# Maxout from two weight differences: the first product goes to the output through w1 @ w_out, and the weights arrive as fp32

## The chip, the cores and the metric

The kernel runs on one core of one Trainium2 chip. The metric is the device time of one execution in microseconds (us). The engines are named as the profile names them: PE does the matrix multiplies (PEld is its weight load, which overlaps them), DVE is the vector engine, ACT the scalar engine, POOL the GpSimd, SP the engine that here only issues DMAs. Each engine works through its own queue in order, so an instruction that waits holds up all that is queued behind it on that engine.

## The reference

A gated linear attention with a recurrent state per head, then a feed-forward layer with three gates of which the largest is kept:

```
for t in range(768):                                   # 4 batches, 8 heads, head_dim 48
    state = alpha[t][:, None] * state + outer(k[t], v[t])
    y[t] = q[t] @ state
x = y as 3072 tokens x 384
h = max(max(x @ w1, x @ w2), x @ w3)                   # w1, w2, w3: 384 x 768
out = h @ w_out                                        # w_out: 768 x 384
```

All inputs and the output are fp32 in HBM.

## The kernel before

The work is cut into 12 steps (`NS`): three chunks of 256 tokens for each of four batches, step s being chunk s // 4 of batch s % 4. A step has two parts. The first is the recurrence in chunked form: load alpha, k, q and v of the step (384 KB each, into four rings of four buffers), logarithms and running sums of alpha, k and q scaled by the decays (`near_k`, `near_q`, `scaled`), transposes, scores, masked scores, the state update and the output y, kept in fp16 as `xT`. The second is the feed-forward part on `xT`: `gate` makes the products with w1, w2 and w3 for a group of 256 of the 768 columns (piece G with index 3 * group + g), `maxed` (piece h) folds them: g = 0 is a copy out of PSUM on ACT or DVE, g = 1 and g = 2 are each a maximum on DVE. `project` (O) multiplies by w_out and `store` (o) scales and sends out.

The order of all this is not found by a scheduler: `emit` runs through the string `ORDER`, one piece after the other, and every engine gets its instructions in that order. A piece is a letter, an index, possibly a letter for the engine (v DVE, p POOL, a ACT) and, behind the @, the step: `w0v@2` is `near_q` of step 2 on DVE. Loads (`l`) go out from SP's queue, or from ACT's with an a; stores and the DMA transposes (`D`) also from SP's. The weights come by piece K (`load_weight`, lines 102 to 109): nine loads of three 128 x 256 blocks of w1, w2, w3 and three of two 128 x 384 blocks of w_out, issued by POOL, which turn fp32 into fp16 on the way into `wcat` and `wo16`. H pieces are warm-up multiplies at the start. PSUM is eight banks, all of one tag.

Pieces that the prediction speaks of: K (`load_weight`), G (`gate`), h (`maxed`), O (`project`), w (`near_q`, `qa` in the profile), k and q (`scaled`, `qk`), S and s (state update `sps` and its sum `full`), z (`kept`), y (`st`), V (`vt`), Y (`attend`, `yps`), r (`inverse`, `ra`).

Of the kernel before, what the change touches and what calls it, by code (L numbers as in the profile page):

```python
# [23 lines left out]
def kernel(  # L24
# [29 lines left out]
    NQ = 4  # L54
    assert DM == H * D and NT == B * S and 2 * D == 3 * C and DM % P == 0
# [32 lines left out]
    wcat = cpool.tile([P, NF, 3, DF], FP16, name="wcat")  # L88
# [13 lines left out]
    def load_weight(_, i, *__):  # L102
        if i < 9:
            w = (moe_w1, moe_w2, moe_w3)[i % 3]
            src = w.rearrange("(f p) j -> p f j", p=P)[:, :, i // 3 * 2 * P:(i // 3 + 1) * 2 * P]
            nc.gpsimd.dma_start(wcat[:, :, i % 3, i // 3 * 2 * P:(i // 3 + 1) * 2 * P], src)
        else:
            src = moe_w_out.rearrange("(j p) m -> p j m", p=P)[:, 2 * (i - 9):2 * (i - 8)]
            nc.gpsimd.dma_start(wo16[:, 2 * (i - 9):2 * (i - 8)], src)
# [42 lines left out]
    def times(eng, dst, src, col):  # L152
# [6 lines left out]
     lps_of, dec_of, tps_of, aps_of, sps_of, gps_of, ops_of, full_of, kept_of) = ({} for _ in range(20))  # L159
# [211 lines left out]

    def gate(s, i, _):
        jg, g = i // 3, i % 3
        xT = xT_of[s]
        gps = bank([P, 2, U * P], f"gps{g}")
        for j in range(2):
            jj = 2 * jg + j
            for f in range(NF):
                nc.tensor.matmul(gps[:, j, :], wcat[:, f, g, jj * P:(jj + 1) * P],  # L379
                                 xT[:, f].rearrange("p u t -> p (u t)"),  # L380
                                 start=(f == 0), stop=(f == NF - 1))
        gps_of[s, i] = gps

    def maxed(s, i, eng):
        jg, g = i // 3, i % 3
        gps = gps_of.pop((s, i))
        if g < 2:
            h = work.tile([P, 2, U * P], FP16, name=f"h{g}", tag=f"h{g}")
# [10 lines left out]
    whole, left, right = slice(0, DM), slice(0, DM // 2), slice(DM // 2, DM)  # L399
    parts = {  # L400
        0: (0, range(NJ), {0: whole}), 1: (1, range(NJ), {1: whole}),
        2: (0, range(4), {0: whole}), 3: (0, range(4, NJ), {0: whole}),
        4: (1, range(4), {1: left, 2: right}), 5: (1, range(4, NJ), {1: left}), 6: (1, range(4, NJ), {2: right}),
    }

    def project(s, x, tag):
        u, jjs, outs = parts[x]
        for o, cols in outs.items():
            if jjs[0] == 0:
                ops_of[s, o] = bank([P, cols.stop - cols.start], "ops")  # L410
            for jj in jjs:
                nc.tensor.matmul(ops_of[s, o], hT_of[s][:, jj, u * P:(u + 1) * P], wo16[:, jj, cols],  # L412
                                 start=(jj == 0), stop=(jj == NJ - 1))

    def store(s, x, eng):
        c, b = divmod(s, B)
        u, cols = (1, (left, right)[x - 1]) if s == NS - 1 and x > 0 else (x, whole)
        ob = work.tile([P, DM], FP32, name="ob", tag="ob", bufs=5)[:, :cols.stop - cols.start]
# [4 lines left out]
    def warm(_, n, *x):  # L423
# [11 lines left out]
        "G": gate, "h": maxed, "O": project, "o": store,  # L435
    }

    def emit(order):
# [6 lines left out]
        l0@0 r0@0 H12@0 H4@0 H1@0 m0p@0 N0@0 c0@0 r1@0 l0@1 m0v@1 l2@0 H1@0 r0@1 f0@0 g0@0 H4@0  # L445
        w0p@0 l1@0 u0v@0 q0v@0 N0@1 c0@1 e0@0 l3@0 V0a@0 r1@1 e0@1 f0@1 l0@2 k1v@0 q1v@0 K1p@0
        M0p@0 l2@1 k0p@0 l1@1 K2p@0 K0p@0 k1p@1 m0v@2 w0v@1 H10@0 g0@1 N0@2 S0@0 s0a@0 T1@0
        t1a@0 c0@2 q1v@1 T0@0 z0p@0 f0@2 e0@2 g0@2 q0v@1 H1@0 l3@1 V0a@1 t0v@0 A1@0 A0@0 T1@1
        H2@0 u0v@1 a2@0 k0p@1 S0@1 T0@1 v1a@0 v0p@0 a1@0 a3@0 a0@0 Y0@0 Y2@0 t1v@1 K5p@0 y0p@0
        s0a@1 M0p@1 z0p@1 Y3@0 l0@3 v1a@1 t0v@1 m0v@3 A1@1 A0@1 x0a@0 x1a@0 G1@0 G2@0 l1@2 a2@1  # L450
        v0a@1 K3p@0 y0p@1 Y3@1 K4p@0 k1p@2 u0p@2 a1@1 N0@3 c0@3 a3@1 a0@1 Y0@1 r0@2 r1@2 x0v@1
        Y2@1 x1a@1 l2@2 s1v@0 s1v@1 f0@3 k0p@2 w0v@2 G0@0 l3@2 M0p@2 G1@1 G0@1 G2@1 h0a@0 q1v@2
        T1@2 g0@3 e0@3 h1v@0 V0a@2 S0@2 s0a@2 h0v@1 q0p@2 h1v@1 T0@2 t0a@2 t1v@2 G5@1 G5@0 K6p@0
        z0p@2 y0a@2 s1v@2 l0@4 v1p@2 h2v@0 h2v@1 r0@4 A1@2 A0@2 a0@2 G3@1 h3a@1 Y3@2 m0p@4 l3a@3
        a3@2 G3@0 N0@4 a1@2 K7p@0 v0p@2 l1@3 r0@3 G4@1 c0@4 g0@4 a2@2 Y2@2 x1v@2 h3a@0 Y0@2
        x0a@2 u0p@3 h4v@1 l0@5 G4@0 h5v@1 M1p@0 z1p@0 y1a@0 G0@2 h0a@2 G5@2 r1@3 G1@2 G3@2 h4v@0
        h5v@0 h1v@2 G2@2 l2@3 K8p@0 k0p@3 w0v@3 q0v@3 G6@2 V0a@3 h3a@2 l2@4 l1@4 r1@4 m0p@5
        M0p@3 h2v@2 G4@2 h4v@2 k1p@3 S0@3 s0v@3 N0@5 G6@1 h6a@2 h5v@2 r0@5 G7@2 h7v@2 T0@3 q1p@3
        T1@3 G7@1 K11p@0 z0p@3 e0@4 w0p@4 f0@4 l3@4 s1v@3 v0a@3 t1v@3 t0a@3 k1v@4 G6@0 h6a@1
        q1p@4 h7v@1 l2@6 u0p@4 c0@5 A0@3 a0@3 A1@3 T1@4 q0p@4 a2@3 G8@2 a3@3 h8v@2 G8@0 g0@5  # L460
        h6a@0 a1@3 f0@5 G8@1 K9p@0 k0p@4 T0@4 e0@5 h8v@1 G7@0 v1p@3 Y0@3 Y2@3 t1a@4 V0a@4 t0a@4
        h7v@0 K10p@0 y0p@3 Y3@3 x0a@3 x1a@3 l1@5 v1p@4 S0@4 A0@4 s0v@4 a1@4 A1@4 a3@4 M0p@4
        z0p@4 s1v@4 u0p@5 G0@3 l0@6 a0@4 G7@3 l1a@6 a2@4 v0v@4 y0a@4 m0p@6 r0@6 G3@3 h3a@3 G1@3
        G6@3 Y0@4 r1@5 l3a@5 h0v@3 Y3@4 h8v@0 Y2@4 x1v@4 N0@6 Y1@4 x0a@4 l2@5 G8@3 M1v@1 c0@6
        e0@6 f0@6 G0@4 h1v@3 k0v@5 q1v@5 G3@4 w0v@5 q0v@5 M0p@5 g0@6 u0v@6 r1@6 G1@4 l0@7 m0v@7
        G2@4 k1p@5 D1@5 h0a@4 z1p@1 k0p@6 O0@1 h1v@4 w0v@6 D0@5 q0p@6 D0@6 k1p@6 q1p@6 O1@1 N0@7
        l0@8 h6a@3 l3@6 h2v@4 l2@7 l1a@7 o1a@1 h7v@3 D1@6 h3v@4 o0a@1 V0a@5 O0@2 o0a@2 O1@2
        y1p@1 G7@4 h8v@3 S0@5 A0@5 s0v@5 o1a@2 a0@5 a1@5 A1@5 a3@5 a2@5 v1a@5 z0p@5 G4@4 v0p@5
# [6 lines left out]
        V0a@7 v1a@7 G0@6 h5v@5 M1v@4 z1p@4 G8@5 h2v@5 h3a@6 h7v@5 h4v@6 S0@7 h0a@6 v0p@7 l3@11
        o1a@0 h8v@5 y1a@4 A0@7 a1@7 s0v@7 u0p@8 A1@7 a2@7 m0p@9 a3@7 M0p@7 z0p@7 y0p@7 k0p@8
        Y1@7 a0@7 r0@9 l1a@9 G2@6 G1@6 h1v@6 q1p@8 G6@6 h6v@6 s1v@7 G5@6 Y0@7 Y2@7 N0@9 l2@9
        m0v@10 w0v@8 q0p@8 D0@8 Y3@7 k1v@8 D1@8 x0a@7 x1a@7 l3@9 G8@6 G7@6 r1@9 G6@7 h6a@7 G0@7
        V0v@8 c0@9 e0@9 O1@3 g0@9 M1p@5 u0v@9 k0v@9 O0@3 f0@9 w0p@9 G4@7 q1p@9 k1p@9 D1@9 q0p@9
        D0@9 o1a@3 o0a@3 V0a@11 h2v@6 h5v@6 h7v@6 h8v@6 G8@7 G7@7 h7v@7 h0a@7 S0@8 N0@10 s0v@8  # L480
# [6 lines left out]
        V0v@10 q0v@10 k0p@10 D0@10 O0@4 O1@4 g0@11 v0a@10 h7v@8 h2v@8 G4@9 h8v@8 G5@8 O1@7 r1@11
        v1p@10 S0@10 h3a@9 h4v@9 o0a@4 o1a@4 q1p@11 k1v@11 o1a@7 M1p@7 D1@11 s0v@10 A0@10 a0@10
        A1@10 a3@10 u0p@11 k0p@11 G7@9 z0p@10 y0a@10 y1p@6 G8@9 G3@8 h3a@8 O0@7 a1@10 w0v@11
        a2@10 h7v@9 h8v@9 Y3@10 Y1@10 Y0@10 Y2@10 G1@9 G0@9 x1v@10 x0a@10 G4@10 z1p@7 q0p@11  # L490
        D0@11 h4v@8 h0a@9 h5v@8 h1v@9 G2@9 G3@10 o0a@7 v1p@11 h2v@9 S0@11 s0v@11 A0@11 A1@11
# [43 lines left out]
```

## Time and profile before

| | us |
|---|---|
| median of 3 runs (152.74, 155.6, 153.05) | 153.05 |
| span of the profiled execution, first to last instruction | 150.5 |
| PE busy in it | 138.6 (92%) |
| DVE busy | 122.2 (81%) |
| ACT busy | 95.4 (63%) |
| POOL busy | 95.0 (63%) |

The profile is of one execution. Its span is 2.55 us below the median of the runs; that part lies before the first and after the last instruction. DMA moved 30.08 MB in 73033 packets, 65456 of them under 512 B; HBM reads are 23.69 MB. The 16 DMA engines are at 90% or more in most slices up to 47 us and again, less evenly, from 60 to 115 us. Names of tiles stand for what is computed: `gps<-xT,wcat` is a gate's product, `h` and `hT` are the folded gates, `ops<-wo,hT` the projection, `rq<-in_q_dram` a load of q.

### The profile page before, as it was taken

To read this page: it belongs to the slowest core of one execution; us is meant where nothing else is said; L and a number is where in the kernel's file an instruction comes from. 1 tells how busy PE (TensorE), PEld (TensorE's weight loads), DVE (VectorE), ACT (ScalarE), POOL (GpSimd) and SP (SyncE) were. 2 spreads that over 40 slices of the span, in tenths; PEclk is the share of its full clock that TensorE was granted. 3 is DMA by queue.
4 is the path that set the end of the run, shared out by engine and by line. 5 is a ranking of instruction groups with operands and counts; after the bars stand their busy time and mean duration, and the time that the engine had idled before them with its cause. 6 is when DMAs were issued, how large, how long until landed. Compare 5 with 4: busy or idle time off the path is not lost.

```text
span 150.5 us, 5517 instructions
## 1 busy us (share of the span) xinstructions
PE 138.6 (92%) x2301; PEld 105.9 (70%) x2301; DVE 122.2 (81%) x224; ACT 95.4 (63%) x199; POOL 95.0 (63%) x155
## 2 busy tenths in 40 slices
PE   6997589999798799999999999999899999999990
PEld 2445368778586588688886887678677788878660
DVE  5279788989999499999996999999699999566620
ACT  3588599575797576785969936788637344313071
POOL 8593999999779891799570976946589921000000
PEclk9999999999999999999999999999999999999998
DMA  5999999999996752999997996999996970011163
GB/s 127 319 317 278 263 239 278 250 271 271 283 248 155 103 135 80 193 227 284 214 245 182 332 331 163 201 178 339 281 246 158 146 95 31 4 52 57 52 235 131
DMA packets 73033, 30.08 MB, mean 200 GB/s; under 512 B 65456, under 2 KB 73008, under 8 KB 73008
## 3 DMA queue, kind: packets, MB, share of 16 engines
q1 hardware_dynamic: 59984, 24.12, 66.2%
q0 software_dynamic: 4416, 2.36, 11.9%
q10 hardware_dynamic: 8608, 3.25, 8.7%
q8 instruction: 18, 0.29, 0.8%
q14 instruction: 7, 0.06, 0.1%
HBM read 23.69 MB, written 4.72 MB: 189 GB/s over the span
## 4 chain that ended last, share of the span: by engine, by line
PE 49%; POOL 16%; DVE 9%; DMA 8%; issue 6%; SPq 5%; ACT 4%; POOLq 0%; DVEq 0%; ACTq 0%
PE gps L379 28%; PE ops L412 13%; POOL qk L222 5%; SPq L95 5%; DMA ra<-in_alpha_dram 4%; DMA rk<-in_k_dram 4%; PE yps L297 4%; DVE qa L193 3%; POOL st L150 2%; DVE h L396 2%; POOL kept L363 2%; PE aps L277 2%; POOL vu L150 2%; DVE hT L396 2%; POOL ka L189 2%
## 5 line engine op out<-in xcount | busy, mean ns | idle before, releaser
L379 PE MATMUL gps<-xT,wcat 128*128 128x256 f16 x648 | 76.5, 273 | 1.5 <-DVE hT L396 0.9
L379 PEld LDWEIGHTS <-wcat 128*128 128x128 f16 x648 | 61.5, 98 | 11.2 <-issue 1.9
L284 DVE TENSOR_TENSOR lat<-aps,cp 128x512 f16<-128x512 f32 x48 | 30.3, 681 | 0.7 <-PE aps L277 0.6
L396 DVE TENSOR_TENSOR h<-gps,h 128x512 f16<-128x512 f32 x36 | 24.6, 684 | 2.7 <-PE gps L379 1.2
L396 DVE TENSOR_TENSOR hT<-gps,h 128x512 f16<-128x512 f32 x36 | 24.1, 684 | 2.0 <-PE ops L412 1.3
L412 PE MATMUL ops<-wo,hT 128*128 128x384 f16 (+1 forms) x150 | 25.2, 320 | 0.0
L148 ACT CAST h<-gps 128x512 f16<-128x512 f32 x28 | 16.3, 584 | 9.1 <-PE gps L379 7.3
L412 PEld LDWEIGHTS <-hT 128*128 128x128 f16 x150 | 14.2, 98 | 7.8
L154 ACT ACTIVATE ob<-ops,c 128x384 f32<-128x384 f32 (+1 forms) x23 | 12.1, 567 | 11.5 <-PE ops L412 11.4
L363 POOL TENSOR_TENSOR kept<-full,gm 128x192 f32<-128x192 f32 x18 | 9.5, 532 | 11.1 <-DVE gm L335 5.0
L150 POOL COPY vu<-vt 64x384 f16<-64x384 f16 x24 | 12.2, 509 | 4.3 <-ACT vt L154 2.8
L148 ACT CAST xT<-yps 128x384 f16<-128x384 f32 x17 | 7.8, 480 | 8.4 <-PE yps L297 8.3
L154 ACT ACTIVATE vt<-rv,c 128x768 f16<-128x768 f32 x10 | 9.4, 940 | 4.9 <-DMA rv<-in_v_dram 4.9
L222 POOL TENSOR_TENSOR qk<-ka,ic 128x384 f16<-128x384 f32 x10 | 10.6, 1056 | 2.9 <-DVE ka L189 2.6
L426 PE MATMUL wps<-wo 128*128 128x512 f16 x35 | 10.6, 455 | 1.2 <-DVE wo L502 1.2
L148 ACT COPY vu<-vt 64x384 f16<-64x384 f16 x22 | 11.2, 509 | 0.3
L222 POOL TENSOR_TENSOR qk<-rq,ac 128x384 f16<-128x384 f32 x8 | 8.0, 998 | 1.5 <-DMA rq<-in_q_dram 1.4
L189 POOL TENSOR_TENSOR ka<-rk,ra 128x384 f32<-128x384 f32 x8 | 8.3, 1040 | 0.2
L277 PE MATMUL aps<-qkT 48*64 48x128 f16 x384 | 7.7, 219 | 0.8 <-DVE qkT L150 0.8
L148 ACT CAST st<-kept 64x192 f16<-64x192 f32 x18 | 6.3, 348 | 3.3 <-POOL kept L363 3.1
L297 PE MATMUL yps<-lat,vu 128*32 128x128 f16 x384 | 8.1, 220 | 0.1
L212 ACT ACTIVATE ac<-lps 128x384 f32<-128x384 f32 x12 | 6.0, 499 | 3.4 <-PE lps L200 3.4
(57 smaller groups left out, 194.6 us busy)
## 6 DMA issues: line engine op xcount, KB each, us to landing
ra<-in_alpha_dram SPq DMA_DIRECT2D x12, 384.0 KB, 5.5
out_dram<-ob SPq DMA_DIRECT2D x23, 192.0 KB, 2.1
rq<-in_q_dram SPq DMA_DIRECT2D x11, 384.0 KB, 6.2
rv<-in_v_dram SPq DMA_DIRECT2D x9, 384.0 KB, 6.6
rk<-in_k_dram SPq DMA_DIRECT2D x8, 384.0 KB, 7.0
wcat<-in_moe_w_dram POOLq DMA_DIRECT2D x9, 192.0 KB, 6.6
rk<-in_k_dram ACTq DMA_DIRECT2D x4, 384.0 KB, 4.4
rv<-in_v_dram ACTq DMA_DIRECT2D x3, 384.0 KB, 4.2
```

What stands on the lines that cost most here:

```text
L148: nc.scalar.copy(out=dst, in_=src)
L150: engines[eng].tensor_copy(out=dst, in_=src)
L154: nc.scalar.mul(dst, src, col)
L189: engines[eng or "p"].tensor_mul(near_of[s, "k"], raw("k", s, 0), raw("a", s, 1))
L222: engines[eng or "p"].tensor_mul(dst.rearrange("p a b c -> p (a b) c")[:, :, :D], near_of.pop((s, n)) if r == 0 else raw(n, s, r), dec_of[ ...
L277: nc.tensor.matmul(aps[i][r * J:(r + 1) * J, a * U + x, :], qkT[rows, r, 1, p, cols], qkT[rows, :, 0, p, cols], start=True, stop=True)
L284: nc.vector.tensor_mul(lat_of[s, u][:, i], aps_of[s, u][i], pmask.unsqueeze(1).broadcast_to([P, HP, P]))
L297: nc.tensor.matmul(y_of[s, x][C * m:C * (m + 1), f, :], lhs, rhs, start=(s, x, m) not in begun, stop=last[x] and n == len(todo) - 1)
L363: engines[eng or "p"].tensor_mul(kept, full_of.pop((s, x)), gm_of.pop((s, x)).unsqueeze(2).broadcast_to([P, HP, D]))
L379: nc.tensor.matmul(gps[:, j, :], wcat[:, f, g, jj * P:(jj + 1) * P], xT[:, f].rearrange("p u t -> p (u t)"), start=(f == 0), stop=(f == NF ...
L396: nc.vector.tensor_max(h, gps, h_of[s, i - 1])
L412: nc.tensor.matmul(ops_of[s, o], hT_of[s][:, jj, u * P:(u + 1) * P], wo16[:, jj, cols], start=(jj == 0), stop=(jj == NJ - 1))
```

## The change

Since max(a, b, c) = a + max(0, b - a, c - a), the output is x @ (w1 @ w_out) + max(0, x @ (w2 - w1), x @ (w3 - w1)) @ w_out. The change computes it so:

- `gate` has two products in place of three for each group of columns, with the differences in `wdif`; pieces G and h now have the index 2 * group + g.
- `maxed`: g = 0 is a positive part (Relu on ACT, maximum with 0 on DVE) instead of a copy, g = 1 one maximum on DVE; the third step is gone.
- `project` adds three products with `xT` and `w1o` ahead of the six with `hT` and `wo16`.
- `w1o` = w1 @ w_out is made on chip: 18 transposes of w1 (pieces B), three copies out of PSUM on DVE (n), 18 multiplies (P), three copies on ACT (p). They stand together just ahead of the first projection.
- the weights are loaded as fp32 from SP's queue into a pool `wst` of five buffers (`NW`), at the places in `ORDER` where POOL issued them before. The six differences are computed by DVE (three) and POOL (three), pieces d; ACT turns w1 and w_out into fp16 (b and C).
- buffers: `xT` 8 in place of 3, `h` 5 in place of two tags of 2, `ob` 4 in place of 5.

In `ORDER`, the pieces other than G, h and the new ones stand in the same sequence as before, on the same engines; of G and h those of the second gate (indices 1, 4, 7) are taken out and the others keep their sequence and engines. Pieces d stand just ahead of the first gate that needs them.

```diff
-    wcat = cpool.tile([P, NF, 3, DF], FP16, name="wcat")
+    wdif = cpool.tile([P, NF, 2, DF], FP16, name="wdif")
+    w1h = cpool.tile([P, NF, DF], FP16, name="w1h")
+    w1T = cpool.tile([P, NJ, DM], FP16, name="w1T")
+    w1o = cpool.tile([P, NF, DM], FP16, name="w1o")
...
-    def load_weight(_, i, *__):
+    def load_weight(_, i, eng):
+        staged = staged_of[i] = work.tile([P, 2 * NF * P], FP32, name="wst", tag="wst", bufs=NW)
         if i < 9:
             w = (moe_w1, moe_w2, moe_w3)[i % 3]
-            src = w.rearrange("(f p) j -> p f j", p=P)[:, :, i // 3 * 2 * P:(i // 3 + 1) * 2 * P]
-            nc.gpsimd.dma_start(wcat[:, :, i % 3, i // 3 * 2 * P:(i // 3 + 1) * 2 * P], src)
...
+            queues[eng].dma_start(staged.rearrange("p (f j) -> p f j", f=NF),
+                                  w.rearrange("(f p) j -> p f j", p=P)[:, :, i // 3 * 2 * P:(i // 3 + 1) * 2 * P])
...
+    def differ(_, i, eng):
+        jg, g = divmod(i, 2)
+        engines[eng or "p"].tensor_sub(
+            wdif[:, :, g, column_group(jg)], staged_of[3 * jg + 1 + g].rearrange("p (f j) -> p f j", f=NF),
+            staged_of[3 * jg].rearrange("p (f j) -> p f j", f=NF))
+
+    def halve(_, i, eng):
+        copy(eng or "a", w1h[:, :, column_group(i)], staged_of[3 * i].rearrange("p (f j) -> p f j", f=NF))
+
+    def turn_weight(_, i, tag):
+        wps_of[i] = bank([P, 2, NF, P], "tps", FP16)
+        for j in range(2):
+            for f in range(NF):
+                nc.tensor.transpose(wps_of[i][:, j, f], w1h[:, f, (2 * i + j) * P:(2 * i + j + 1) * P], ident)
+
+    def keep_weight(_, i, eng):
+        copy(eng or "v", w1T[:, 2 * i:2 * i + 2].rearrange("p j m -> p (j m)"),
+             wps_of.pop(i).rearrange("p j f m -> p (j f m)"))
+
+    def halve_out(_, i, eng):
+        copy(eng or "a", wo16[:, 2 * i:2 * i + 2].rearrange("p j m -> p (j m)"), staged_of[9 + i])
+
+    def multiply_weights(_, f, tag):
+        pps_of[f] = bank([P, DM], "pps")
+        for j in range(NJ):
+            nc.tensor.matmul(pps_of[f], w1T[:, j, f * P:(f + 1) * P], wo16[:, j], start=(j == 0), stop=(j == NJ - 1))
+
+    def keep_product(_, f, eng):
+        copy(eng or "a", w1o[:, f], pps_of.pop(f))
...
     def maxed(s, i, eng):
-        jg, g = i // 3, i % 3
+        jg, g = divmod(i, 2)
...
-        if g == 0:
-            copy(eng or "a", h, gps)
+        if g == 0 and eng == "v":
+            nc.vector.tensor_scalar_max(h, gps, 0.0)
+        elif g == 0:
+            nc.scalar.activation(out=h, in_=gps, func=AFT.Relu)
         else:
             nc.vector.tensor_max(h, gps, h_of[s, i - 1])
...
+    every = direct + through
...
-            for jj in jjs:
-                nc.tensor.matmul(ops_of[s, o], hT_of[s][:, jj, u * P:(u + 1) * P], wo16[:, jj, cols],
-                                 start=(jj == 0), stop=(jj == NJ - 1))
+            for what, j in terms:
+                lhs = xT_of[s][:, j, u] if what == "x" else hT_of[s][:, j, u * P:(u + 1) * P]
+                nc.tensor.matmul(ops_of[s, o], lhs, (w1o if what == "x" else wo16)[:, j, cols],
+                                 start=((what, j) == every[0]), stop=((what, j) == every[-1]))
```

The part of `ORDER` in which the new pieces first appear, before and after (`d`, `b` and the K without p are new; line breaks moved):

```
before: ... x0a@0 x1a@0 G1@0 G2@0 l1@2 a2@1 v0a@1 K3p@0 y0p@1 Y3@1 K4p@0 k1p@2 u0p@2 ... r0@2 r1@2 x0v@1 Y2@1 x1a@1 l2@2
        s1v@0 s1v@1 f0@3 k0p@2 w0v@2 G0@0 l3@2 M0p@2 G1@1 G0@1 G2@1 h0a@0 q1v@2 T1@2 ... G5@1 G5@0 K6p@0 ... l0@4 ...
after:  ... x0a@0 x1a@0 d1p@0 G1@0 l1@2 a2@1 v0a@1 K3@0 y0p@1 Y3@1 K4@0 k1p@2 u0p@2 ... r0@2 r1@2 x0v@1 Y2@1 x1a@1 l2@2
        s1v@0 s1v@1 f0@3 k0p@2 w0v@2 d0v@0 b0a@0 G0@0 l3@2 M0p@2 G0@1 G1@1 h0a@0 q1v@2 T1@2 ... d3p@0 G3@1 G3@0 K6@0 ... l0@4 ...
```

More of the change, by code (lines that the diff above doesn't have):

```diff
@@ L378, in gate @@
             for f in range(NF):
[L379 removed]
+                nc.tensor.matmul(gps[:, j, :], wdif[:, f, g, jj * P:(jj + 1) * P],
                                  xT[:, f].rearrange("p u t -> p (u t)"),
@@ L457 @@
[L457 to L468, printed above, removed]
@@ L475 @@
[L475 to L480, printed above, removed]
@@ L487 @@
[L487 to L491, printed above, removed]
-        a0@11 a3@11 h3a@10 G6@10 G0@10 M0p@11 z0p@11 G5@9 G1@10 y0v@11 a1@11 y1a@7 Y1@11 Y3@11
@@ new lines @@
+        h1v@5 h2a@6 S0@7 h0a@6 v0p@7 l3@11 o1a@0 h5v@5 y1a@4 A0@7 a1@7 s0v@7 u0p@8 A1@7 a2@7 m0p@9 a3@7
+        M0p@7 z0p@7 y0p@7 k0p@8 Y1@7 a0@7 r0@9 l1a@9 G1@6 q1p@8 G4@6 h4v@6 s1v@7 G3@6 Y0@7 Y2@7 N0@9 l2@9
+        m0v@10 w0v@8 q0p@8 D0@8 Y3@7 k1v@8 D1@8 x0a@7 x1a@7 l3@9 G5@6 r1@9 G4@7 h4a@7 G0@7 V0v@8 c0@9 e0@9
+        O1@3 g0@9 M1p@5 u0v@9 k0v@9 O0@3 f0@9 w0p@9 q1p@9 k1p@9 D1@9 q0p@9 D0@9 o1a@3 o0a@3 V0a@11 h1v@6
+        h3v@6 h5v@6 G5@7 h0a@7 S0@8 N0@10 s0v@8 O0@5 o0a@5 A0@8 a0@8 A1@8 a2@8 l0@11 Y1@8 G2@7 v1a@8 h2a@7
@@ new lines @@
+        O1@7 r1@11 v1p@10 S0@10 h2a@9 o0a@4 o1a@4 q1p@11 k1v@11 o1a@7 M1p@7 D1@11 s0v@10 A0@10 a0@10 A1@10
+        a3@10 u0p@11 k0p@11 z0p@10 y0a@10 y1p@6 G5@9 G2@8 h2a@8 O0@7 a1@10 w0v@11 a2@10 h5v@9 Y3@10 Y1@10
+        Y0@10 Y2@10 G0@9 x1v@10 x0a@10 z1p@7 q0p@11 D0@11 h0a@9 h3v@8 G1@9 G2@10 o0a@7 v1p@11 h1v@9 S0@11
+        s0v@11 A0@11 A1@11 a0@11 a3@11 h2a@10 G4@10 G0@10 M0p@11 z0p@11 G3@9 y0v@11 a1@11 y1a@7 Y1@11 Y3@11
+        v0a@11 a2@11 Y0@11 Y2@11 G1@10 x0a@11 G5@10 x1a@11 G5@11 G3@10 h3v@9 G3@11 h4a@10 h0v@10 G0@11
```

98 lines of the change are left out of this document (55 added, 43 removed).

## The prediction

> **What bounds the kernel now.** I read the page first, then the stretches of 5 us, then each queue in order of time. On the page PE leads, with the gates ahead of all else:
>
> ```profile
> PE 138.6 (92%) x2301; PEld 105.9 (70%) x2301; DVE 122.2 (81%) x224; ACT 95.4 (63%) x199; POOL 95.0 (63%) x155
> ```
>
> A mean over the span hides two regimes, which the stretches show (columns: PE, PEld, DVE, ACT, POOL, clock, DMA share, GB/s):
>
> ```profile
> 25.00:30.00 5.00, 4.73 (x106) 3.80 (x103) 4.97 (x9) 3.45 (x8) 4.86 (x7) 1.00 1.21 252
> 35.00:40.00 5.00, 4.41 (x69) 3.82 (x67) 4.96 (x5) 3.05 (x7) 4.98 (x7) 1.00 1.28 260
> ...
> 85.00:90.00 5.00, 5.00 (x93) 4.19 (x86) 5.00 (x10) 2.70 (x7) 4.30 (x8) 1.00 1.16 335
> 130.00:135.00 5.00, 5.00 (x43) 3.90 (x41) 2.19 (x4) 0.58 (x1) 0.00 (x0) 1.00 0.04 14
> ```
>
> Up to about 51 us (the front) DVE, POOL and the DMA engines are full and PE has gaps; from there PE has no gap in nearly every stretch, at a granted clock of 1.00. The chain of waits says where the front hands over (start, us, what), and gives the pace of PE:
>
> ```profile
> 50.86 0.35 POOL st L150
> 51.21 0.04 issue
> 51.26 0.35 PE yps L297 x11
> ...
> 91.64 1.97 PE ops L412 x12
> ...
> 134.25 4.58 PE gps L379 x42
> ```
>
> At 51.26 PE gets step 3's state from POOL. A gate multiply streams in 4.58/42 = 0.109 us, a projection multiply in 1.97/12 = 0.164.
>
> **PE's work.** 36 gate pieces of 6 multiplies go: 216 x 0.109 = 23.5 us. Added: three projection multiplies for each of 23 whole outputs and, for the halves, 6 half-wide ones (0.082): 69 x 0.164 + 0.5 = 11.8; 18 multiplies for w1 @ w_out, 3.0; 18 transposes at 0.46/8 = 0.058, 1.0. Over the whole kernel that is -7.7 us. But where it falls decides. Up to that point in `ORDER` the old program has 27 gate pieces and the new one 18, and none of the added work: 5.9 us leave the front, where PE already waits, so I count them at nothing. Behind it 27 pieces go, 17.7 us, and 15.8 come. The PE-bound part gains **1.9 us**, not 7.7. DVE loses 36 maxima of 0.684 (24.6 us); 27 of them lie where PE sets the time, so worth nothing.
>
> **The front.** Two things move here. DVE is relieved of 9 maxima (issued some 0.6 apart, 5.4 us) and gets three differences. POOL loses 12 DMA issues (7.3 + 2.3 = 9.6 us) and gets three differences of 768 columns, by its 384-column product (1.00) some 2.0 each. Alone that would make the front shorter. The other thing is SP. Its queue before (start, us until the issue was through):
>
> ```profile
> 14.21 4.02 SPq L95 DMA_DIRECT2D rq<-in_q_dram  x1
> 18.28 1.07 SPq L95 DMA_DIRECT2D rv<-in_v_dram  x1
> 19.53 1.00 SPq L95 DMA_DIRECT2D ra<-in_alpha_dram  x1
> ```
>
> The reader is to see that SP issues without a pause, held only by the DMA engines: a load takes about 1.2 us and all loads of the front are queued one behind the other until 44.8. Now weight loads stand in that queue and five staging buffers hold them. K1, K2, K0, K5, K3 take the five; K4 needs one back, and the first comes back when POOL has made d1. POOL makes d1 behind `kept` of step 1, at about 20.0 (that `kept` ran at 20.16 behind one weight issue more), until 22.0. So SP stands from 18.2 (16 issues at about 1.1) to 22.0, and behind K4 stand q and v of step 2, in the list above at 14.21 and 18.28. With the DMA engines run dry K4 lands at 24.9 (first load: issued 0.74, landed by 4.1 in the packet records) and q of step 2 one load later, 26.1; before it had landed by 21.5. DVE wanted it here:
>
> ```profile
> 24.54 0.82 DVE L193 TENSOR_TENSOR qa<-rq,ra 128x384 f32<-128x384 f32 x1
> 25.28 1.35 DVE L222 TENSOR_TENSOR qk<-rq,ac 128x384 f16<-128x384 f32 x1
> ...
> 37.16 2.83 DVE L193 TENSOR_TENSOR qa<-rq,ra 128x384 f32<-128x384 f32 x1
> ```
>
> So `w0v@2` goes to 26.4, +1.9. Right behind it is d0: its price is not in the trace; the nearest row is DVE's `qa` and `ka` of 384 fp32 columns, 0.55 alone, so 1.0 to 1.1 for 768, and 2.83 for 384 when POOL worked beside it. I take 1.0 here (POOL waits for that same `qa`), with 2.8 as the upper end. K6 waits for d0 (28.1), and behind K6 stand alpha of step 4, then K7, k of step 3, alpha of step 5, q of step 3: these land at about 32.2 to 36.7 instead of 27.6 to 32.7. G0 of steps 0 and 1 waits for d0 too, and with it `T1@2`, which stood at 26.69 and now comes near 30.2. Then d3 on POOL (28.2 to 30.2) holds G3, and d2 on DVE, behind the first masked scores of step 2 (about 35), holds G2. ACT has `h2a@1` behind G2, and behind that the load of v of step 3 (issued at 31.00 before, about 36.6 now) and `r1@3`, so `w0v@3` comes near 41 instead of 37.16 (it had waited for POOL until 40). By there DVE has been spared the maxima, which brings back most: `s0v@3` (41.71 before) comes near 43.8. The POOL chain from `z0p@3` (42.21) to `st` is 9.0 us; with d5 (+2.0) and without three issues of 0.76 (-2.3) and with one wait of DVE less sure it stays 9.0 to 9.4. The hand-over moves by 2.1 + 0.3 = **+2.4 us**. Ends: if the buffers come back in time, DVE's own balance, 5.4 - 3.0 = -2.4; with every difference of DVE at 2.8, +4.5. I take the chain above since each wait in it is written into the queues.
>
> In the page's rows a packet of 1 KB cast to 512 B on POOL's queue costs more than the plain one will (60 ns against 46, between 38 ns at 776 B and 65 at 1536 B in the packet records): 12 loads save some 3 us of DMA time, which the two dry spells of SP, about 2 us each, use up.
>
> [...]
>
> **Product and first projection.** B, n, P, p stand in one row on PE: P waits for DVE's copies (768 columns of fp16, between 0.55 and 0.68 by the rows of 384 and of 1024), and the last of the three comes 1.0 us after the last transpose; O0 waits for the last `p` (0.48 us by `xT`'s copy). With DVE in step that is 0.5 + 0.5 = 1.0 of gap, with DVE as far behind PE as at 60 us (its `ka`, `pa`, `h` run at 59.86 to 61.48, beside PE's projection at 60.19) 2.0 to 3.0. I take **+1.5**. The Relu costs what the copy did (0.584), the three fp16 conversions of ACT per kind (0.94 each by `vt`) lie in ACT's idle time; if ACT were late they would cost 0.9 apiece.
>
> Sum on the span: 150.5 + 2.4 - 1.9 + 1.5 = 152.5; with 2.55 outside the span **155.0 us**.
>
> **Rivals.**
> - *Forecast: the front gets later and eats the gain.* 155.0, own range 152.5 to 157.5. Chance 0.48.
> - *The staging buffers come back in time, or SP's stand stays hidden.* Front 0 to -2.4, product +1.0: 150.5 - 1.9 + 1.0 + 2.55 = 152.2 down to 149.8. For it: DVE is full in the front and loses work. Against: K4's wait on d1. 0.22. [...]
> - *PE sets the whole span.* All of -7.7 comes, product +1.0: 146.4. For it: 92% busy. Against: the gaps of the front. 0.08.
> - *The middle becomes bound by the recurrence, slower.* Counted piece by piece, PE's work between 51 us and the last output of step 11 (128 us) falls by 4.2 and rises by 2.3 behind it, where only PE works (POOL 0.00 at 130). If POOL's and SP's chain of step 5 to 11 paces the middle, the 4.2 turns into waiting and only the tail's +2.3 is left: 155.0 + 4.2 = 159.2. It makes the kernel slower by over 2% from 1.1 us of new gaps on. For it: SP waits 18.5 us for DVE ahead of its transposes; against: POOL is at 63% and DVE is relieved of 18 us there. 0.22.
>
> A measurement of this kernel can tell about 2% from no change, 149.99 to 156.11. Faster: all of the third, a tenth of the second and little else, 0.11. Slower: the fourth less a little, 0.20, and the upper part of the forecast, 0.14, makes 0.34. Same 0.55. The range for 8 in 10 leaves out the third case and the upper half of the fourth: 149.8 to 159.0.
>
> **What would show it.** Gate rows: 432 of about 273 ns; SP's queue with a stand of some 4 us ahead of the load of K4 that ends with POOL's first `wdif`, and one ahead of K6 that ends with DVE's; `rq` of step 2 as what DVE waits for near 26; PE's handover from POOL's `st` near 53.7; PE gaps of 1 to 2 us between the `w1T` copies and the first `ops`. Wrong it is if the chain has no SP or staging wait before 51 us, if DVE's `wdif` rows are far from 1.0, or if PE shows new gaps of over 2 us between 65 and 125 us.

## The result and the profile after

| | before | after |
|---|---|---|
| median of 4 runs, us | 153.15 (152.74 to 155.6) | 171.02 (170.5 to 171.18) |
| span of the profiled execution | 150.5 | 169.2 |
| mean granted clock of PE in it | 0.995 | 0.935 |

The ratio is 1.1182, with a 95% interval of 1.1149 to 1.1215: slower by 17.9 us. Some executions run some per cent longer than the others of their kernel, like the one of 155.6 here: the ratios and the medians of the experiments below leave them out, and a mark that is read from the profile of such an execution carries a ≤. PE does hardly more than before and all others but ACT do less, as the page of the profile shows (engine, busy us, share of the span, instructions), and the second line, the granted clock in 40 slices, has low stretches from 17 to 34 us and near 48 and 61:

```profile
PE 139.7 (83%) x2196; PEld 99.6 (59%) x2196; DVE 109.8 (65%) x194; ACT 100.9 (60%) x208; POOL 93.7 (55%) x146
...
PEclk9999567599978969999999999999999999999998
```

So the 18.7 us of the span are not added work: PE waits longer and, where its clock is low, takes longer for the same. To find where, I cut both spans at three marks that every version has: the end of the copy `xT` of step 3 (first half; the end of the front), that of step 5, and that of step 11. Before, then after (columns as in the stretches shown with the prediction):

```profile
0.00:50.60 50.60, 43.59 (x727) 31.20 (x727) 41.68 (x81) 36.48 (x74) 42.92 (x70) 1.00 1.10 249
50.60:69.50 18.90, 18.47 (x376) 14.74 (x377) 16.83 (x33) 12.53 (x28) 13.90 (x24) 1.00 0.77 166
69.50:128.60 59.10, 58.51 (x1061) 46.56 (x1059) 53.89 (x96) 39.99 (x87) 38.13 (x63) 1.00 0.95 209
128.60:150.50 21.90, 18.05 (x142) 13.44 (x140) 9.85 (x16) 6.36 (x13) 0.00 (x0) 0.97 0.25 91
```

```profile
0.00:62.60 62.60, 44.24 (x725) 30.54 (x729) 39.97 (x75) 40.04 (x80) 42.44 (x65) 0.84 0.85 242
62.60:86.70 24.10, 21.37 (x358) 15.04 (x347) 16.80 (x33) 14.45 (x33) 12.14 (x18) 1.00 0.73 185
86.70:145.00 58.30, 53.79 (x983) 39.82 (x981) 47.14 (x78) 39.89 (x87) 39.11 (x63) 1.00 0.79 186
145.00:169.20 24.20, 20.32 (x151) 14.23 (x149) 5.84 (x10) 6.56 (x13) 0.00 (x0) 0.97 0.23 82
```

The four stretches change by +12.0, +5.2, -0.8 and +2.3 us. The reader is to see two things. In the front PE's busy time is the same (43.6 and 44.2) and the length is not: it waits 18.4 us instead of 7.0. The busy time is the same although 54 gate multiplies fewer lie in it (108 instead of 162; at 0.109 they are 5.9 us), since the clock there is 0.84 instead of 1.00. In the third stretch, with the clock at 1.00 in both, PE's busy time falls by 4.7 us and the length by 0.8: PE had no gap there before, and lost work there bought almost nothing.

In the front the chain of waits shows the steps that the prediction spoke of, one after the other (start, us, what):

```profile
21.88 1.78 POOL wdif L384
...
23.67 0.37 SPq L112
...
24.08 4.15 DMA rq<-in_q_dram
...
28.33 0.06 DVE qa L200
...
28.80 0.96 DVE wdif L384
...
29.81 4.02 PE gps L419 x18
33.83 0.85 PE tps L263 x8
...
47.35 0.96 DVE wdif L384
...
48.35 1.46 PE gps L419 x6
49.82 0.61 PE sps L355 x18
...
55.52 1.81 POOL wdif L384
...
57.38 2.98 PE gps L419 x18
```

SP stands until POOL has made the first difference, and q of step 2 goes out only then. Three more differences, two of DVE and one of POOL, lie on the chain, each followed at once by a row of gates on PE, and the transposes (`tps`) and state products (`sps`) of the recurrence come behind those gates. The gates are slow, too: 18 multiplies in 4.02 us are 0.223 each, where the trace of before had 0.109, and PE's clock in stretches of 2.5 us says why:

```profile
17.50:20.00 2.50, 0.12 (x9) 0.12 (x12) 1.25 (x3) 1.08 (x2) 1.42 (x5) 0.51 1.11 307
20.00:22.50 2.50, 2.50 (x84) 2.25 (x83) 0.98 (x2) 2.43 (x6) 1.13 (x2) 0.50 0.72 207
22.50:25.00 2.50, 2.50 (x62) 1.68 (x52) 2.50 (x3) 2.26 (x6) 2.36 (x4) 0.62 0.11 20
```

The clock falls to a half at 17.55 us, in a stretch with 0.12 us of work, and stays there until 24.4 us (and again from 27.8 to 34.6, 48.3 to 51.7 and 58.5 to 61.9 us). The three rows of gates on the chain, 42 multiplies, take 4.02 + 1.46 + 2.98 = 8.46 us; at 0.109 each they would take 4.58, so 3.9 us of the chain are the low clock. The row at 22.50 also shows the DMA engines run dry (20 GB/s) while SP stands.

### The profile page after: what moved, and what is told of

Its sections match the earlier page's. It is cut to its first block, busy times and chain, and to the rows that moved or that the text cites. A ratio compares the mean times of both kernels' runs of the same rounds, so it can differ in the third digit from the quotient of the medians.

```text
span 169.2 us, 5268 instructions
## 1 busy us (share of the span) xinstructions
PE 139.7 (83%) x2196; PEld 99.6 (59%) x2196; DVE 109.8 (65%) x194; ACT 100.9 (60%) x208; POOL 93.7 (55%) x146
## 4 chain that ended last, share of the span: by engine, by line
PE 29%; DMA 19%; DVE 14%; ACT 12%; POOL 9%; issue 8%; SPq 7%; ACTq 0%; POOLq 0%; DVEq 0%
PE ops L458 13%; PE gps L419 10%; DMA rv<-in_v_dram 7%; DMA rq<-in_q_dram 6%; SPq L99 5%; DMA qkT<-qk 4%; DVE lat L291 3%; DMA ra<-in_alpha_dram 3%; POOL qk L229 3%; ACT vu L155 2%; SPq L112 2%; POOL wdif L384 2%; PE pps L407 2%; DVE qa L200 2%; ACT vt L161 2%
## 5 line engine op out<-in xcount | busy, mean ns | idle before, releaser
L419 PE MATMUL gps<-xT,wdif 128*128 128x256 f16 x432 | 56.9, 287 | 10.8 <-DVE wdif L384 7.2
L419 PEld LDWEIGHTS <-wdif 128*128 128x128 f16 x432 | 42.1, 102 | 20.2 <-DVE wdif L384 7.8
L458 PE MATMUL ops<-wo,hT 128*128 128x384 f16 (+1 forms) x150 | 27.5, 320 | 0.0
L436 ACT ACTIVATE h<-gps 128x512 f16<-128x512 f32 x28 | 16.4, 594 | 10.0 <-PE gps L419 8.9
L458 PE MATMUL ops<-w1o,xT 128*128 128x384 f16 (+1 forms) x75 | 16.0, 320 | 0.2 <-ACT w1o L155 0.2
L304 PE MATMUL yps<-lat,vu 128*32 128x128 f16 x384 | 9.2, 234 | 3.2 <-DVE vu L157 1.7
L284 PEld LDWEIGHTS <-qkT 48*64 48x64 f16 x384 | 6.4, 111 | 6.5 <-DVE qkT L157 2.3
L229 POOL TENSOR_TENSOR qk<-rq,ac 128x384 f16<-128x384 f32 x8 | 9.3, 1161 | 1.5 <-DMA rq<-in_q_dram 1.4
L304 PEld LDWEIGHTS <-vu 128*32 128x32 f16 x384 | 6.7, 104 | 4.7 <-DVE vu L157 1.9
L458 PEld LDWEIGHTS <-xT 128*128 128x128 f16 x75 | 6.9, 98 | 3.3
```

The source lines that it names most:

```text
L229: engines[eng or "p"].tensor_mul(dst.rearrange("p a b c -> p (a b) c")[:, :, :D], near_of.pop((s, n)) if r == 0 else raw(n, s, r), dec_of[ ...
L284: nc.tensor.matmul(aps[i][r * J:(r + 1) * J, a * U + x, :], qkT[rows, r, 1, p, cols], qkT[rows, :, 0, p, cols], start=True, stop=True)
L304: nc.tensor.matmul(y_of[s, x][C * m:C * (m + 1), f, :], lhs, rhs, start=(s, x, m) not in begun, stop=last[x] and n == len(todo) - 1)
L419: nc.tensor.matmul(gps[:, j, :], wdif[:, f, g, jj * P:(jj + 1) * P], xT[:, f].rearrange("p u t -> p (u t)"), start=(f == 0), stop=(f == NF ...
L436: nc.scalar.activation(out=h, in_=gps, func=AFT.Relu)
L458: nc.tensor.matmul(ops_of[s, o], lhs, (w1o if what == "x" else wo16)[:, j, cols], start=((what, j) == every[0]), stop=((what, j) == every[ ...
```

## The experiments

Five causes were to be told apart: the staging through SP; the gates that wait for a difference at the head of PE's queue (in some expectations theory D is its form in which the order alone decides); the half clock; the time of the differences themselves on POOL and DVE; and, behind the front, the product w1 @ w_out against a middle that PE does not pace. The marks of all kernels, in us of the span of the profiled execution; the last column is the median, the number of executions that it is taken from and, where there is one, the 95% interval of the ratio to before.

| | `xT` of step 3 | of 5 | of 11 | span | median (executions; ratio, 95%) |
|---|---|---|---|---|---|
| before | 50.6 | 69.5 | 128.6 | 150.5 | 153.05 (3) |
| after | 62.6 | 86.7 | 145.0 | 169.2 | 171.02 (4; 1.1149 to 1.1215) |
| e1_cast16 | 59.5 | 84.0 | 143.3 | 167.5 | 169.14 (2) |
| e2_warm | ≤62.8 | ≤86.8 | ≤144.1 | ≤168.3 | 167.48 (1) |
| e3_noprod | 62.0 | 80.6 | 140.8 | 165.2 | 166.93 (2; 1.0791 to 1.1033) |
| e4_beforeprod | 50.7 | 74.3 | 133.6 | 155.5 | 157.35 (2; 1.0172 to 1.04) |
| e5_front3 | 50.7 | 71.9 | 132.7 | 156.9 | 159.6 (4; 1.0399 to 1.051) |
| e6_late | 61.0 | 85.0 | 145.5 | 169.7 | 170.86 (2; 1.1096 to 1.1272) |
| e7_late16 | 63.8 | 88.1 | 149.7 | 174.0 | 174.76 (2; 1.1332 to 1.1546) |
| e8_twogates | 49.8 | 69.1 | 126.9 | 146.2 | 148.32 (4; 0.9654 to 0.9841) |
| e9_pack | ≤51.0 | ≤73.5 | ≤133.6 | ≤157.8 | 157.4 (3; 1.0238 to 1.0427) |
| e10_nowait | 56.1 | 82.2 | 142.7 | 167.0 | 168.71 (2; 1.0996 to 1.1128) |
| e11_latediff | 51.6 | 77.8 | 138.6 | 162.9 | 165.69 (2; 1.0726 to 1.095) |
| e12_beforediff | ≤56.1 | ≤77.3 | ≤137.1 | ≤159.0 | 158.14 (1) |

**The staging (e1_cast16).** The weights go back to POOL's queue and are turned into fp16 on the way, w1 into `w1h`, w2 and w3 into `wdif`, where the differences are made in place; the pieces b and C of ACT fall away.

```diff
-            queues[eng].dma_start(staged..., w...)
+            dst = w1h[...] if i % 3 == 0 else wdif[:, :, i % 3 - 1, column_group(i // 3)]
+            nc.gpsimd.dma_start(dst, w...)
...
-        tensor_sub(wdif[...], staged_of[3 * jg + 1 + g]..., staged_of[3 * jg]...)
+        tensor_sub(wdif[...], wdif[...], w1h[...])
```

> The weights arrive as before (POOL's queue, fp32 to fp16 on the way, no staging buffers); the two differences are taken in fp16, in place; ACT's conversions fall away; gates, product and projections are those of the changed kernel. Theory A (the front's 9 us come from fp32 weights in SP's queue behind five buffers, and what hangs on it): SP shows no stand before 45 us, the hand-over of step 3's state falls from 60.2 to 50 to 52 us, and the time to 157 to 162 us. Rival B (PE's clock, granted at about half in the front, would fall without the staging too): the clock rows stay at 0.5 to 0.8 between 20 and 35 us and the time stays above 165. Rival C (the product and the middle take most of the 18 us): the front is back but the time is 163 or more.

The front ends at 59.5 instead of 62.6: the staging, with all that goes with it, is worth 3.1 us, and 1.9 of the whole. The run does not single out SP's stand: the differences also get shorter in fp16 (DVE's 0.95 to 0.55, the first one 1.35; POOL's 1.81 to 1.63), ACT is spared its conversions, and POOL issues the loads again. It is the cause that the prediction had at its centre, and a quarter of the loss in the front. The clock fell without the staging too, to 0.67 from 20 to 25 us and 0.81 from 30 to 35 us, as rival B had it.

**The clock (e2_warm).** Warm-up multiplies are put ahead of the gates that wait, so that PE has something to do there.

```diff
-H2@0 ... G0@0 ... G2@1 ... G4@2 ... G4@1
+H14@0 ... H12@0 G0@0 ... H8@0 G2@1 ... H12@0 G4@2 ... H9@0 G4@1
```

> The changed kernel with warm-up multiplies put into the gaps that PE has ahead of S0 of step 1 and of the gates that wait for differences (12 more there, 12, 8, 12, 9; they add PE work and change no result). Rival B: the granted clock stays near 1.0 up to 65 us, 18 gate multiplies ahead of T1 of step 2 take 2.0 us instead of 4.0, and the time falls by 3 to 6 us, to 165 to 168. Theory A: the clock recovers but the waits on staged loads remain, so it falls by at most 3 us.

In the profiled execution (170.13 us) the mean clock rose from 0.935 to 0.970, though it was still 0.80 from 20 to 25 us and 0.78 from 30 to 35, and the front ended where it had, at 62.8. Between the copies of steps 1 and 3 it took 32.5 us instead of 35.1, but the added multiplies, which stand in PE's queue like all else, had cost the same ahead of that. The other execution, at a clock of 0.990, took 167.48, 3.5 us less than after; it has no profile. What the half clock costs thus stays open: 2.6 us in that part, 3.5 in the time, or the 3.9 by which it lengthens the gates on the chain. Where work fills the gaps, this run can't tell the clock from its cure.

**The product (e3_noprod, e4_beforeprod).** The first leaves the product out of after (first diff; pieces B, n, P, p; `w1o` is zero, so the output lacks the first product). The second adds it to before (second diff), its result unused.

```diff
-z1p@1 k0p@6 B0@0 B1@0 B2@0 n0v@0 n1v@0 n2v@0 P0@0 p0a@0 P1@0 p1a@0 P2@0 p2a@0 O0@1
+z1p@1 k0p@6 O0@1
```

```diff
-z1p@1 k0p@6 O0@1
+z1p@1 k0p@6 B0@0 B1@0 B2@0 n0v@0 n1v@0 n2v@0 P0@0 p0a@0 P1@0 p1a@0 P2@0 p2a@0 O0@1
```

> The changed kernel without w1 @ w_out: pieces B, n, P and p are left out and w1o is set to zero, so the first product's share of the output is left out. PE loses 18 transposes and 18 multiplies (3.9 us at full clock), DVE three copies, ACT three. If the product stands on the path with its waits, as forecast (3.9 + 1.5): 165 to 166 us. If the recurrence paces PE there anyway: 168 to 171.

> The kernel before with the product alone added at the same place (its result is not used): w1 from the fp16 weights, transposes, copies, multiplies. PE sets the time there, so at least its work of 3.9 us shows, and with the wait between B and P 4.5 to 6 us: 157.5 to 159. If DVE and ACT were the bound there: 154 to 156.

Without it the second stretch takes 18.6 us instead of 24.1, and the kernel 4.1 less; with it before takes 23.6 there instead of 18.9, and 157.35 against 152.53 in the same comparison, 4.8 more. The chain of after shows what it is made of: copies and multiplies that hand over to one another, the first output only behind them.

```profile
71.96 0.48 DVE w1T L157
...
72.49 3.39 PE pps L407 x18
...
75.90 0.49 ACT w1o L155
```

e3_noprod tells something else as well. From the end of the front to step 11 it has 140.8 - 62.0 = 78.8 us; before had 128.6 - 50.6 = 78.0. It has a third less of the gates, and three more products for each half of an output, and is not shorter.

**The order on PE (e6_late, e7_late16).** The recurrence's pieces are put ahead of the gates that wait for a difference, in after and in e1_cast16. The differences on DVE are moved back with their gates, and the load of v of step 3 goes out ahead of them.

```diff
-w0v@2 d0v@0 b0a@0 G0@0 l3@2 M0p@2 G0@1 G1@1 h0a@0 q1v@2 T1@2 ... T0@2
+w0v@2 b0a@0 l3@2 M0p@2 q1v@2 d0v@0 T1@2 ... T0@2 G0@0 G0@1 G1@1
...
-q0v@3 d4v@0 G4@2 V0a@3 ... S0@3 s0v@3 N0@5 G4@1 ... T0@3 q1p@3 T1@3
+q0v@3 V0a@3 ... S0@3 s0v@3 d4v@0 N0@5 ... T0@3 q1p@3 T1@3 G4@2 G4@1
```

> The changed kernel, staging and all, with the order alone altered in the front: gates of steps 0 to 2 that wait for a difference are put behind the recurrence pieces that stood behind them on PE (G1 of step 0 behind x of step 1; G0, G1 behind T0 of step 2; G3 behind A0 of step 2; G2 behind x of step 2; G4 behind T1 of step 3), the differences on DVE behind q, x and s in the same way, and the load of v of step 3 ahead of them. Theory D: the hand-over falls from 60.2 to 53 to 56 us (what the staging alone costs by the forecast is 2.4) and the time to 163 to 167. If the staged loads set the front: it stays above 58 and the time above 168.

> The same order as the last kernel with the weights by POOL's queue in fp16 and no staging, as in the first experiment. The difference to the last kernel is what SP's staged loads cost once the gates no longer hide it. Forecast's staging term: 2 to 3 us less than the last kernel, hand-over 51 to 53 us, time 161 to 165. If staging costs nothing at all: the same within 1 us.

This did not help: 61.0 and 63.8 at the end of the front, times of 170.86 and 174.76. By its own expectation e6_late would say that the staged loads set the front, but e7_late16, which has none, is 3.9 us slower still, which neither expectation had. The gates no longer stood ahead of the recurrence on PE, and the clock fell further, to 0.50 to 0.52 from 20 to 35 us in e6_late. In e7_late16 one difference met a run of POOL's instructions (DVE's queue, then the first and last of POOL's run: start, us, line, operation, tiles):

```profile
38.74 4.89 DVE L383 TENSOR_TENSOR wdif<-wdif,w1h 128x768 f16<-128x768 f16 x1
```

```profile
39.22 1.00 POOL L228 TENSOR_TENSOR qk<-ka,ic 128x384 f16<-128x384 f32 x1
...
42.23 0.98 POOL L228 TENSOR_TENSOR qk<-rq,ac 128x384 f16<-128x384 f32 x1
```

DVE's subtraction, 0.55 us at two of its three places in e1_cast16, lasts from 38.74 to 43.63, just past the end of POOL's run at 43.21. The order of PE alone was not the cause. Nor is what a wait at the head of PE's queue costs shown by these two runs, since the differences moved with the gates.

**The wait and the work of the differences (e10_nowait, e12_beforediff, e11_latediff).** e10_nowait is e1_cast16 with w2 and w3 in a tile of their own: the gates of steps 0 to 2 read them and wait for no difference, while the differences are still made at their places (for those steps the output has the raw gates). e12_beforediff is before with the six differences added at the same places, unused. e11_latediff is e10_nowait with all six on DVE: two of them early, in DVE's own gaps, the others later, at 43.4, 53.9, 57.1 and 59.2 us. The diffs stand in this order; of `ORDER` each shows a piece d with the piece beside it.

```diff
-                nc.tensor.matmul(gps[:, j, :], wdif[:, f, g, jj * P:(jj + 1) * P],
+                nc.tensor.matmul(gps[:, j, :], (w23 if s < 3 else wdif)[:, f, g, jj * P:(jj + 1) * P],
```

```diff
+        engines[eng or "p"].tensor_sub(wdif[:, :, g, cols], wcat[:, :, g + 1, cols], wcat[:, :, 0, cols])
...
+d1p@0 l1@2 ... d0v@0 l3@2 ... d3p@0 z0p@2 ... d2v@0 Y3@2 ... d4v@0 V0a@3 ... d5p@0 a3@3
```

```diff
-d1p@0 G1@0 ... d0v@0 G0@0 ... d3p@0 G3@1 ... d2v@0 G2@1 ... d4v@0 G4@2 ... d5p@0 G5@2
+d0v@0 t0v@1 ... d1v@0 x0v@1 ... d2v@0 k1v@4 ... s1v@4 d4v@0 ... v0v@4 d5v@0 ... x1v@4 d3v@0
```

> The first experiment's kernel (fp16 weights, no staging, two gates in every step) with one thing altered: the gates of steps 0 to 2 read the raw w2 and w3 instead of the differences (the subtraction is left out of these steps), so they need not wait for them; the differences are still made at the same places. Theory D1 (the waits on differences hold the recurrence): hand-over at 51 to 54 us and the time at 160 to 163 though PE has no more work in the front than in the changed kernel. Rival D2 (it is the missing work: PE idles without the third gate and its clock falls, whatever it waits for): the clock still falls to 0.5 to 0.8 and the hand-over stays above 57.

> The kernel before with the six differences alone added (fp16, from its fp16 weights, three on POOL, three on DVE, at the places in the order that they have in the changed kernel; the result is not used). All gates stay and none waits for a difference. If the differences' own time on POOL and DVE delays the recurrence of the front: x of step 3 at 53 to 56 us instead of 50.6 and 155 to 158. If DVE and POOL take them in their gaps: within 1 us of the kernel before.

> The last kernel but one of the same call's predecessor (gates of steps 0 to 2 read raw w2 and w3, so the subtraction is left out there; fp16 weights, two gates, no staging), with the six differences moved: all on DVE, two into gaps before 24 us, four behind 45 us, as in the fifth experiment. If the time that the differences take on DVE and POOL inside the front is what was left of the delay (x of step 3 at 56.1 there, 50.6 before): x of step 3 at 50 to 52.5 us and the time 3 to 6 us lower, 163 to 166. If it was the falling clock or the missing third gate: x of step 3 stays above 55 and the time above 167.

Taking the wait away brings the front from 59.5 to 56.1, 3.4 us, and the clock in the front from 0.86 to 0.94; the mark lies between what D1 and D2 expected. Of these 3.4 us only 0.4 remain in the time (168.71 against 169.14). The 5.5 us left over before are the differences' own: e12_beforediff, which has all three gates and nothing that waits for the differences, ends its front at 56.1 as well at most (its time is 5 us above before's), and e11_latediff, which differs from e10_nowait in nothing but who makes them and where, at 51.6; 3.0 of these 4.5 us remain in its time (165.69 against 168.71). So the front is not the whole loss: e11_latediff has it back but for 1.0 us and is still 8.4% slower than before. Its second stretch takes 26.2 us where before has 18.9, 5.5 of that by the product; the other 1.8 are not explained. The chain of e10_nowait shows how the differences get in although no gate waits for them:

```profile
44.00 0.55 DVE wdif L384
...
50.82 1.63 POOL wdif L384
...
53.18 1.00 POOL qk L229
```

The last one lies between two of POOL's instructions for the recurrence and moves the second by its whole length.

**The front given back (e5_front3, e9_pack).** e5_front3 keeps the algebra but lets steps 0 to 2 use three gates as before, in the order of before, with two of the differences in DVE's gaps, at 18.5 and 22.8 us, and four from 49.5 us on; the product is made ahead of the first output that needs it, its transposes before `O1@0`. The weights come as in e1_cast16. e9_pack has the product's pieces earlier and spread out between those of the recurrence of steps 4 and 5, and its first copies on ACT.

```diff
-        jg, g = divmod(i, 2)
+        jg, g = divmod(i, 3 if s < 3 else 2)
...
-                nc.tensor.matmul(gps[:, j, :], wdif[:, f, g, jj * P:(jj + 1) * P],
+                nc.tensor.matmul(gps[:, j, :], (w1h[:, f, jj * P:(jj + 1) * P] if s < 3 and g == 0 else
+                                                 w23[:, f, g - 1, jj * P:(jj + 1) * P] if s < 3 else
+                                                 wdif[:, f, g, jj * P:(jj + 1) * P]),
...
+        if s < 3:
+            terms = through
```

> Steps 0 to 2, whose gates fill PE in the front, take their three gates from w1, w2 and w3 as the kernel before (weights by POOL's queue as before, six-term projections for these steps); from step 3 on the differences are used, taken on DVE long before the first gate that needs them; the product stands later, its copies ahead of the sixth projection pair. Theory D (in PE's queue the recurrence of steps 2 and 3 stands behind gates that wait for differences, and PE idles and loses its clock there): the hand-over of step 3's state is back at 51 to 52 us, the clock at 1.0 throughout, and the time falls by 9 us and more, to 155 to 160. Rival B' (the half clock alone): the same time, but then the warm kernel should have gained most of it, which it did not. Rival E (the recurrence paces the middle: steps 5 to 11 take 59 us in every kernel so far): from the end of step 5's x to that of step 11's again 59 us, so that less PE work there brings nothing; if PE paced it, 54 to 56 us.

> The kernel with three gates in steps 0 to 2 (fifth experiment), with the product put into gaps that PE has there: transposes ahead of Y0 of step 4 (a gap of 1.5 us at 55.6), the copies on ACT instead of DVE, the multiplies ahead of S0 and A0 of step 5 (gaps of 0.6 and 1.4 us). If the product costs what does not fit into gaps: 2.5 to 3.5 us less than that kernel, 155 to 157. If the recurrence around it takes the time anyway: the same within 1 us. Either way above the kernel before.

The front of e5_front3 is before's, 50.7 us, and its mean clock there is 1.00. It takes 159.6 us all the same: what is left of the change behind the front costs 4.5%. e9_pack, at 157.4, is the fastest version of the algebra found here, 2.2 us below e5_front3 where 2.5 to 3.5 had been expected. No version that beats before was found, and this was no search.

**Who paces the middle (e8_twogates).** Before, with the products with w2 left out in all steps (pieces G and h 1, 4 and 7 are out of `ORDER`, the output is made from the larger of two, `h0` has 5 buffers); no work is added.

```diff
-            nc.vector.tensor_max(h, gps, h_of[s, i - 1])
+            nc.vector.tensor_max(h, gps, h_of[s, i - 2])
```

> The kernel before with the second gate left out (the products with w2 and their maxima, indices 1, 4 and 7 of each step; h0 gets five buffers so that they last to the third gate), nothing else: PE loses 23.5 us of work and DVE 24.6. If PE paced the kernel behind the hand-over, the 17.7 us behind it go: 135 to 138. Theory E (the recurrence paces the middle as closely as PE did): the front stays at 50.5 to 52, x of step 5 to x of step 11 stays at 57 to 59 us, only the gates behind the last output go (8.5 / 3 = 2.8 us) and a little before: 148 to 151.

216 multiplies (23.5 us of PE at before's pace) and 36 maxima (24.6 us of DVE) go, and the time falls from 152.34 in the same comparison to 148.32, by 4.0. Of the 4.3 us on the span 0.8 lie in the front, 1.3 in the third stretch, 2.6 behind step 11, where POOL is done (and 0.4 are lost in the second). In the third stretch PE now has 6.2 us of idle time where it had 0.6:

```profile
69.10:126.90 57.80, 51.57 (x953) 37.86 (x951) 45.21 (x78) 39.63 (x87) 38.77 (x61) 0.94 0.88 210
```

So in a middle in which PE was busy at 99% something else took nearly as long. The chain of before does not show it, since it runs along PE there (gates are 40% of it between 69 and 130 us). The low clock in this row, 0.94, is not what held the length: e5_front3 has 1.00 in its third stretch, PE idle for 4.6 us, and takes 60.8 us. The chain of after points to what it may be (start, us, what):

```profile
116.97 0.58 ACT ob L161
...
120.26 0.14 SPq L467
...
120.45 5.72 DMA rq<-in_q_dram
...
126.23 1.00 POOL qk L229
...
137.28 3.20 DMA qkT<-qk
...
140.52 0.44 PE aps L284 x15
```

SP sends out a scaled output, then the load of q queued behind that store; POOL scales, a DMA transposes, PE gets its scores. Between the first and the last of these lines, 24 us, the chain has no line of PE, so no gate. Whether loads ahead of the stores would shorten it was not tried.

## Why the prediction was wrong

It forecast 155.0 us with a range to 159.0, and the time was 171.02. On the span the miss is 16.7 us: 9.6 in the front (+12.0 for +2.4; the forecast counted to POOL's `st`, which came 6.5 late, and the mark, the copy of step 3, lies behind it) and 7.1 from there to step 11 (+4.4 for -2.7, which is the fall of 4.2 in PE's work and the +1.5 for the product). The tail, +2.3, came as counted.

**The front, its first steps: right in kind, short in size.** SP stood ahead of K4 until POOL's difference (forecast 22.0, measured 23.67) and ahead of K6 until DVE's; q of step 2 landed at 28.2 (26.1; in before at 21.8); d0 took 0.95 (1.0); `T1@2` came at 33.83 (30.2). These are late by 1.7 to 3.6 us. The first 1.7 come in part from v of step 1, which with three weight loads now ahead of it in SP's queue landed at 18.9 (before 16.8); 2.0 of the 3.6 are the gates ahead of `T1@2`, 18 in 4.02 us, which the forecast had put at the full clock. That "SP issues without a pause, held only by the DMA engines" is not what the profile of before says: it puts 13.8 us of SP's waits up to 48 us down to POOL, ACT and DVE. The step back to POOL's queue in e1_cast16, with all that it changes, gave 3.1 us; that this is near the forecast's +2.4 is chance, since that number was a sum of other terms.

**The front, the step that failed: "By there DVE has been spared the maxima, which brings back most".** This was the term that took the forecast from 41 us for `w0v@3` back to 43.8 for `s0v@3`, 2.1 us later than before; they came at 44.80 and 50.41, 7.6 and 8.7 later. So the 1.7 us that were to come back between the two did not, and 1.1 more were lost. The relief of DVE by 5.4 us was counted, but DVE's load was not what the chain ran through. Two prices were missing. A gate that waits for its difference holds the state products and transposes that stand behind it in PE's queue: 3.4 us (e1_cast16 against e10_nowait; the clock is in it, and the two runs with another order did not bring it back). The prediction named the waits of G0, G2 and G3, and `T1@2` behind the first, but not `S0@3` (the `sps` at 49.82 in the chain above), which stood behind G4, nor `T0@4` and `Y0@3`, which stood behind G5 until 60.36, so that the copy of step 3 comes 3 us later against the hand-over than before (PE's queue: start, us, what, and in brackets the idle time before it and what ended it):

```profile
48.35 1.46 PE L419 MATMUL gps<-xT,wdif 128*128 128x256 f16 x6 [2.80 <-DVE wdif L384]
```

And six differences were put between the recurrence's own instructions on POOL and DVE, at a moment when those engines pass work back and forth: 5.5 us (e10_nowait against before, net of what two gates instead of three save; with e11_latediff for the place). The forecast priced single ones rightly (1.8 to 2.1 on POOL for 2.0, 0.95 on DVE for 1.0) and took them as paid by the spared maxima and DMA issues. The three parts, 3.1, 3.4 and 5.5, are those of one order of undoing them; in another order they might divide otherwise. They are lengths of the front, not of the time: of the 11.0 us that e11_latediff has back there, 5.3 show in its time. The last stretch, from `z0p@3` to `st`, was right again: 9.3 us for 9.0 to 9.4. The end of the range for the front, +4.5, came from raising the durations of DVE's differences to 2.8, and those were not the trouble.

**The middle: rival 4 came true and more.** "From there PE has no gap" was read as "PE sets the time". Of the fall in PE's work up to step 11 nothing came (e3_noprod: 78.8 us for 78.0), as that rival had it with 4.2 us; the trace even held what spoke for it, and it was given 0.22. The test by removal (e8_twogates) makes it plain: 99% busy and 89% busy (51.57 of 57.80) took the same time within 1.3 us. Which chain it is that takes as long, the rival's of POOL and SP or another, was not tested by a run of its own.

**The product: right in its sum.** 4.0 us of work and 1.5 of gaps make 5.5, which were 5.5 in its stretch (e3_noprod; 4.6 of PE's busy time and 0.9 of gaps) and 4.1 to 4.8 in the whole time; e3_noprod loses part of its gain again in the third stretch, which takes 60.2 us instead of 58.3.

**What would show it.** Gate rows of 273 ns at the median, 432 of them: so it was. The hand-over from POOL's `st` stood at 60.2, not 53.7. Of the signs that would make it wrong, "new gaps of over 2 us between 65 and 125 us" was the right one to name; they came as many small ones, 4.5 us in the third stretch.

## What to carry to other kernels

An engine without gaps need not be what sets the time (PE was busy at 99% in the third stretch of before, which with a third of the gates gone got shorter by 1.3 us): take work away from it and look at the length of the stretch before counting a saving on it. New work in a front where engines pass a recurrence back and forth can cost most of its length at the place where it stands, however idle the mean (six differences of 7.4 us in all cost 5.5 in e10_nowait); put it where the trace of that engine has a gap, or behind the hand-over (e11_latediff has 4.5 of them back), and keep what waits for it off the head of a queue that the recurrence needs (3.4 us of the front, e1_cast16 against e10_nowait). Price a wait by everything queued behind it, on the issuing queue (q of step 2 behind SP's wait until 23.67) and on the consumer's (`S0@3` behind G4 until 49.82).

## What the hardware did that was not expected

Between 5 and 165 us PE's granted clock changed in after at 17.55, 24.38, 27.79, 34.62, 48.27, 51.68, 58.51 and 61.92 us, 3.41, 6.83 or 13.65 us apart, each a whole multiple of 3.41. Each fall to a half came behind a stretch of 3.41 us of that grid in which PE was busy for 1.62, 1.73, 0.69 and 1.19 us; stretches with 1.83 (from 65.34 us) and 1.97 (from 10.72) left it at 1.00, and before, on the grid of its one fall at 149.04 us, had no stretch below 2.08 from 5.7 us on until the last one ahead of that fall, which had 1.03. The length of a pause alone does not tell the falls: the first two came 0.8 and 0.7 us after a pause had begun (pauses of 3.11 and 2.67 us), and within pauses of 1.99 us (to 15.15) and 1.74 us (to 39.23) there was none. What decides a fall is not shown by these two profiles. In e8_twogates the mean clock of the front was 0.93, and the front still ended 0.8 us earlier than before; with a third less of the gates there, what the low clock cost it is not shown.

DVE's subtraction of two operands of 768 fp16 columns took 0.55 us at 46.02 us in e1_cast16, where POOL had no instruction but the issue of a DMA from 45.05 to 49.20; 1.35 at 26.95 there, beside POOL's `qk` of 26.62 to 27.87, and 1.35 once each in e10_nowait and e12_beforediff; and 4.89 in e7_late16, beside the run of POOL's instructions shown with that experiment. In e7_late16 DVE's record begins 0.48 us before the first of POOL's two rows shown, in e1_cast16 0.33 us after POOL's, so it is not always the same engine that came first. The cause is not shown.
